# A gated add over 50 MB: loads in one order on one DMA ring, stores held back on the other

## The chip, the cores and the metric

The kernel runs on one core of a Trainium2 chip. Times are device microseconds of one execution; the kernel before takes 121.15 us, the median of 8 runs (120.98 to 121.7). The profile shows one such execution, taken by the hardware profiler, with times counted from its first instruction.

The core's engines that appear here are VectorE (DVE), which does the arithmetic, TensorE (PE), used once, and two engines that only issue transfers: SyncE (SP) and ScalarE (ACT). Each of the two has its own DMA ring, a queue of transfers between the chip's HBM and the core's SBUF. All transfers are carried by the same 16 DMA engines.

## The reference

```python
B, S, D = 1024, 16, 512
x = normal(B, S, D) * 0.05        # bf16
y = normal(B, S, D) * 0.05        # bf16
gamma = 1e-4 * normal(D) * 0.05   # bf16
out = x + gamma * y
```

x, y and the output have 16.78 MB each: two are read, one is written, 50.33 MB in all.

## The kernel before

The 16384 rows of 512 numbers are spread over 128 partitions, 128 consecutive rows (128 KB) to each. All of y has a place in SBUF (`y_sb`, 128 KB per partition). x has two buffers of 32 rows (32 KB per partition each). The work is cut into four pieces of 32 rows per partition; a piece of x, y or the output is one DMA of 4 MB. The result of a piece is written over its y, and stored from there.

First gamma is brought to all partitions: one row is loaded (line 65), TensorE multiplies it by a column of ones into PSUM (line 69), and VectorE copies it to SBUF (line 71).

Then VectorE runs two instructions per piece, in order: y times gamma (line 98), waiting for that piece of y, then x plus the product (line 104), waiting for that piece of x and for the product.

The order of the transfers is written out by hand, and each ring takes its transfers in that order:
- SP's ring: x of pieces 0 and 1 (lines 75, 76), which are put at the very start of the program; after the first add the reload of x for piece 2 (line 78), after the second add that for piece 3 (line 80), directly after it the store of piece 0 (line 81), and after the third add the store of piece 2 (line 83).
- ACT's ring: gamma, then y of all four pieces, without a wait (line 87); after the second add the store of piece 1 (line 91), after the fourth the store of piece 3 (line 93).

Waits go through semaphores; `_take` (line 12) waits for a count and takes it off again. A DMA adds 16 to its semaphore when it has landed. At the end SP waits for the stores of both rings (lines 115, 116). Loads all go through the helper on line 62, so the profile shows them with that line. The profile's q1 is SP's ring, q10 is ACT's.

Of the kernel before, what the change touches and what calls it, by code (L numbers as in the profile page):

```python
# [3 lines left out]

PIECE = 32
MULT, ADD = mybir.AluOpType.mult, mybir.AluOpType.add


def _take(sem, n, eng):


    return eng.wait_ge(sem, n).then_inc(sem, -n)  # L12


def kernel(
    tc: tile.TileContext,
    x: bass.AP,
    y: bass.AP,
    gamma: bass.AP,
    out: bass.AP,  # L20
):

    nc = tc.nc
    P = nc.NUM_PARTITIONS
    tc.close()
    tc.compile()  # L29

    xf = x.flatten_outer_dims()
    yf = y.flatten_outer_dims()
    of = out.flatten_outer_dims()
    N, D = xf.shape
    rows = N // P
    n = rows // PIECE
    dt = xf.dtype
    xv = xf.rearrange("(p n) d -> p n d", p=P)
    yv = yf.rearrange("(p n) d -> p n d", p=P)
    ov = of.rearrange("(p n) d -> p n d", p=P)  # L40

    gamma_row = nc.alloc_sbuf_tensor("gamma_row", [1, D], dt).ap()
    ones_row = nc.alloc_sbuf_tensor("ones_row", [1, P], dt).ap()
    gamma_sb = nc.alloc_sbuf_tensor("gamma_sb", [P, D], dt).ap()
    y_sb = nc.alloc_sbuf_tensor("y_sb", [P, rows, D], dt).ap()
    xs = [nc.alloc_sbuf_tensor(f"x{i}", [P, PIECE, D], dt).ap() for i in range(2)]
    gamma_ps = nc.alloc_psum_tensor("gamma_ps", [P, D], mybir.dt.float32).ap()

    sem = nc.alloc_semaphore
    s_gamma, s_ones, s_ps, s_dve = sem("s_gamma"), sem("s_ones"), sem("s_ps"), sem("s_dve")  # L50
    s_x = [sem(f"s_x{c}") for c in range(n)]
    s_y = [sem(f"s_y{c}") for c in range(n)]
    s_sp, s_act = sem("s_sp"), sem("s_act")
    s_out_sp, s_out_act = sem("s_out_sp"), sem("s_out_act")

    def piece(c):
        return slice(c * PIECE, (c + 1) * PIECE)

    first = []

    def load(eng, dst, src, s):
        return eng.dma_start(out=dst, in_=src).then_inc(s, 16)


    first.append(load(nc.scalar, gamma_row, gamma.unsqueeze(0), s_gamma))
    nc.vector.memset(ones_row, 1.0).then_inc(s_ones, 1)  # L66
    _take(s_ones, 1, nc.tensor)
    _take(s_gamma, 16, nc.tensor)
    nc.tensor.matmul(gamma_ps, ones_row, gamma_row, start=True, stop=True).then_inc(s_ps, 1)  # L69
    _take(s_ps, 1, nc.vector)  # L70
    nc.vector.tensor_copy(out=gamma_sb, in_=gamma_ps).then_inc(s_dve, 1)  # L71
    _take(s_dve, 1, nc.vector)


    first.append(load(nc.sync, xs[0], xv[:, piece(0), :], s_x[0]))
    first.append(load(nc.sync, xs[1], xv[:, piece(1), :], s_x[1]))
    _take(s_sp, 1, nc.sync)
    load(nc.sync, xs[0], xv[:, piece(2), :], s_x[2])
    _take(s_sp, 1, nc.sync)
    load(nc.sync, xs[1], xv[:, piece(3), :], s_x[3])  # L80
    nc.sync.dma_start(out=ov[:, piece(0), :], in_=y_sb[:, piece(0), :]).then_inc(s_out_sp, 16)
    _take(s_sp, 1, nc.sync)
    nc.sync.dma_start(out=ov[:, piece(2), :], in_=y_sb[:, piece(2), :]).then_inc(s_out_sp, 16)


    for c in range(n):
        i = load(nc.scalar, y_sb[:, piece(c), :], yv[:, piece(c), :], s_y[c])
        if c < 2:
            first.append(i)
    _take(s_act, 1, nc.scalar)  # L90
    nc.scalar.dma_start(out=ov[:, piece(1), :], in_=y_sb[:, piece(1), :]).then_inc(s_out_act, 16)
    _take(s_act, 1, nc.scalar)
    nc.scalar.dma_start(out=ov[:, piece(3), :], in_=y_sb[:, piece(3), :]).then_inc(s_out_act, 16)

    for c in range(n):
        yt = y_sb[:, piece(c), :]
        _take(s_y[c], 16, nc.vector)
        nc.vector.tensor_tensor(  # L98
            out=yt, in0=yt, in1=gamma_sb[:, None, :].to_broadcast([P, PIECE, D]), op=MULT
        ).then_inc(s_dve, 1)  # L100
        _take(s_x[c], 16, nc.vector)
        _take(s_dve, 1, nc.vector)

        i = nc.vector.tensor_tensor(out=yt, in0=xs[c % 2], in1=yt, op=ADD)  # L104
        if c == 0:
            i.then_inc(s_sp, 1)
        elif c == 1:
            i.then_inc(s_dve, 1)
            _take(s_dve, 1, nc.vector)
            nc.vector.sem_inc(s_sp, 1)  # L110
            nc.vector.sem_inc(s_act, 1)
        else:
            i.then_inc(s_sp if c == 2 else s_act, 1)

    _take(s_out_sp, 32, nc.sync)
    _take(s_out_act, 32, nc.sync)

    main = nc.main_func.blocks[0].instructions
    names = {i.ins.name for i in first}
    for b in nc.main_func.blocks[1:]:  # L120
        for i in [i for i in b.instructions if i.name in names]:
            b.instructions.remove(i)
    for k, i in enumerate(first):
        main.insert(1 + k, i.ins)


# [1 line left out]
_INS = ['x', 'y', 'gamma']  # L128
_OUTS = [((1024, 16, 512), 'bfloat16')]


# [23 lines left out]
```

## Time and profile before

| what | value |
|---|---|
| median of 8 runs | 121.15 us (120.98 to 121.7) |
| the profiled execution's own time | 121.46 us |
| its span, first to last instruction | 120.1 us |
| VectorE busy | 70.3 us (59%) in 10 instructions |
| one multiply, one add (128 x 16384, bf16) | 8.69 us each, four of each |
| moved by DMA | 50.33 MB, mean 419 GB/s over the span |
| VectorE idle before its first multiply | 18.2 us |

How to read it: a page of the profile lists busy time by engine, then the span in 40 equal slices, where each digit is the busy share of a slice in tenths, then the DMA queues with their packets, megabytes and share of the 16 DMA engines' time. Other views give the instructions in order of time, the busy times and transfer rate in stretches that one names, and the DMA queues of a stretch. Instructions that issue a DMA are shown with the time of the issue alone, and transfers are seen in the DMA rows.

### The profile page before, as it was taken

How to read it: one execution, taken by the hardware profiler on the slowest of the kernel's cores; microseconds unless marked ns; L12 is line 12 of the kernel's file. 1: busy time of each engine (PE TensorE's matmuls, PEld its weight loads, DVE VectorE, ACT ScalarE, POOL GpSimd, SP SyncE). 2: the span in 40 equal slices, each digit the busy share in tenths (PEclk: the TensorE clock that was granted, in tenths of full speed). 3: DMA queues.
4: the chain of work that ended last, by engine and by line, in shares of the span. 5: the costliest groups of instructions: out<-in, count | busy, mean ns of one | idle time of the engine just before them, and what ended most of it. 6: DMA issues, size and time to landing. Idle time of an engine off the chain costs nothing. (4 is left out here: it accounts for less than half of the span.)

```text
span 120.1 us, 90 instructions
## 1 busy us (share of the span) xinstructions
PE 0.6 (0%) x1; PEld 0.1 (0%) x1; DVE 70.3 (59%) x10; POOL 0.2 (0%) x4
## 2 busy tenths in 40 slices
PE   0100000000000000000000000000000000000000
PEld 0000000000000000000000000000000000000000
DVE  0200000099999999999899999899999700000000
POOL 0000000000000000000000000000000000000000
DMA  8999998989898989898989999999999999999994
GB/s 306 393 447 426 426 447 382 491 371 502 360 513 349 524 349 524 349 513 360 491 382 458 415 426 327 426 393 480 393 480 393 469 404 469 393 458 415 436 436 186
DMA packets 1730, 50.33 MB, mean 419 GB/s; under 512 B 193, under 2 KB 194, under 8 KB 194
## 3 DMA queue, kind: packets, MB, share of 16 engines
q1 hardware_dynamic: 864, 25.17, 49.7%
q10 hardware_dynamic: 866, 25.17, 48.7%
HBM read 33.56 MB, written 16.78 MB: 419 GB/s over the span
## 5 line engine op out<-in xcount | busy, mean ns | idle before, releaser
L98 DVE TENSOR_TENSOR y_sb<-y_sb,gamma_sb 128x16384 bf16<-128x16384 bf16 x4 | 34.8, 8690 | 19.2 <-DVEq L12 19.2
L104 DVE TENSOR_TENSOR y_sb<-x,y_sb 128x16384 bf16<-128x16384 bf16 x4 | 34.8, 8692 | 0.6
L71 DVE CAST gamma_sb<-gamma_ps 128x512 bf16<-128x512 f32 x1 | 0.7, 692 | 2.5 <-DVEq L12 2.5
L66 DVE MEMSET ones_row<- 1x128 bf16 x1 | 0.2, 165 | 2.7 <-PEq L29 2.7
L69 PE MATMUL gamma_ps<-gamma_row,ones_row 1*128 1x512 bf16 x1 | 0.6, 577 | 4.6 <-PEq L12 4.6
L69 PEld LDWEIGHTS gamma_ps<-gamma_row,ones_row 1*128 1x128 bf16 x1 | 0.1, 99 | 4.6 <-issue 4.6
L139 POOL MEMSET const-bfloat16-1.0<- 128x1 bf16 x1 | 0.1, 101 | 0.0
L139 POOL MEMSET const-uint8-127<- 128x1 uint8 x1 | 0.1, 101 | 0.0
L139 POOL MEMSET const-float32-0.0<- 128x1 f32 x1 | 0.1, 98 | 0.2 <-issue 0.2
L139 POOL MEMSET const-float32-1.0<- 128x1 f32 x1 | 0.1, 98 | 0.0
## 6 DMA issues: line engine op xcount, KB each, us to landing
x<-in_x_dram SPq DMA_DIRECT2D x4, 4096.0 KB, 24.7
y_sb<-in_y_dram ACTq DMA_DIRECT2D x4, 4096.0 KB, 47.2
out_dram<-y_sb ACTq DMA_DIRECT2D x2, 4096.0 KB, 30.4
out_dram<-y_sb SPq DMA_DIRECT2D x2, 4096.0 KB, 42.3
gamma_row<-in_gamma_dram ACTq DMA_DIRECT2D x1, 1.0 KB
```

The costliest lines, as they stand in the source:

```text
L66: nc.vector.memset(ones_row, 1.0).then_inc(s_ones, 1)
L69: nc.tensor.matmul(gamma_ps, ones_row, gamma_row, start=True, stop=True).then_inc(s_ps, 1)
L71: nc.vector.tensor_copy(out=gamma_sb, in_=gamma_ps).then_inc(s_dve, 1)
L98: nc.vector.tensor_tensor(out=yt, in0=yt, in1=gamma_sb[:, None, :].to_broadcast([P, PIECE, D]), op=MULT).then_inc(s_dve, 1)
L104: i = nc.vector.tensor_tensor(out=yt, in0=xs[c % 2], in1=yt, op=ADD)
L139: nc = _bacc.Bacc("TRN2", target_bir_lowering=False, num_devices=1)
```

## The change

The lists at the top of the file now say what goes where. Rows are counted per partition, of 128.

- Loads go on SP's ring alone, as four of 64 rows (64 KB per partition, 8 MB each): y rows 0 to 63, x rows 0 to 63, y rows 64 to 127, x rows 64 to 127. The first two are at the start of the program. There is one x buffer of 64 rows, as large as the two before; the last load writes over the first x, and so SP waits before it for the adds of pieces 0 and 1.
- Stores go on ACT's ring alone, after gamma: rows 0 to 63 in one DMA of 8 MB, then rows 64 to 95, then rows 96 to 127. The first waits for `s_go`, and each waits for the adds of its rows.
- VectorE's order is now multiply 0, multiply 1, add 0, add 1, multiply 2, multiply 3, go, add 2, add 3. Its pieces still have 32 rows. `go` waits for the open multiplies and raises `s_go`; in the code it stands ahead of the third add.
- One semaphore counts the adds, with waits that don't take it down until the end; one counts all stores, waited for at 48.

The diff, cut to its core:

```diff
-PIECE = 32
+PIECES = [32, 32, 32, 32]
+SP = [('y', 0, 64), ('x', 0, 64, 0), ('y', 64, 128), ('x', 64, 128, 0)]
+ACT = [('g',), ('s', 0, 64), ('s', 64, 96), ('s', 96, 128)]
+EARLY = (2, 1)
+DVE = [('m', 0), ('m', 1), ('a', 0), ('a', 1), ('m', 2), ('m', 3), ('go',), ('a', 2), ('a', 3)]
...
-    xs = [nc.alloc_sbuf_tensor(f"x{i}", [P, PIECE, D], dt).ap() for i in range(2)]
+    x_rows = max(w[3] + w[2] - w[1] for w in x_loads)
+    x_sb = nc.alloc_sbuf_tensor("x_sb", [P, x_rows, D], dt).ap()
...
+    def frees(w):
+        old = x_loads[: x_loads.index(w)]
+        old = [v for v in old if meets(v[3], v[3] + v[2] - v[1], w[3], w[3] + w[2] - w[1])]
+        return [c for v in old for c in pieces_of(v[1], v[2])]
...
+    def ring(eng, what, n_early):
+        known, went = 0, False
+        for k, w in enumerate(what):
+            kind = w[0]
+            need = frees(w) if kind == "x" else pieces_of(w[1], w[2]) + list(w[3:]) if kind == "s" else []
+            need = max((order[c] + 1 for c in need), default=0)
+            if kind == "s" and not went and ("go",) in DVE:
+                _take(s_go, 1, eng)
+                went = True
+            if need > known:
+                eng.wait_ge(s_add, need)
+                known = need
...
+            elif kind == "x":
+                to = x_sb[:, w[3] : w[3] + w[2] - w[1], :]
+                i = eng.dma_start(out=to, in_=xv[:, w[1] : w[2], :]).then_inc(s_load[w], 16)
+            elif kind == "y":
+                r = slice(w[1], w[2])
+                i = eng.dma_start(out=y_sb[:, r, :], in_=yv[:, r, :]).then_inc(s_load[w], 16)
+            else:
+                r = slice(w[1], w[2])
+                i = eng.dma_start(out=ov[:, r, :], in_=y_sb[:, r, :]).then_inc(s_out, 16)
...
+    ring(nc.sync, SP, EARLY[0])
+    ring(nc.scalar, ACT, EARLY[1])
...
+    for kind, *args in DVE:
+        if kind == "go":
+            if open_mults:
+                _take(s_dve, open_mults, nc.vector)
+                open_mults = 0
+            nc.vector.sem_inc(s_go, 1)
+            continue
...
+        if kind == "m":
+            need(y_loads, c)
+            g = gamma_sb[:, None, :].to_broadcast([P, PIECES[c], D])
+            nc.vector.tensor_tensor(out=yt, in0=yt, in1=g, op=MULT).then_inc(s_dve, 1)
+            open_mults += 1
         else:
+            need(x_loads, c)
+            if open_mults:
+                _take(s_dve, open_mults, nc.vector)
+                open_mults = 0
+            at = x_at(starts[c])
+            xt = x_sb[:, at : at + PIECES[c], :]
+            nc.vector.tensor_tensor(out=yt, in0=xt, in1=yt, op=ADD).then_inc(s_add, 1)
+
+    nc.scalar.sem_inc(s_end, 1)
+    _take(s_end, 1, nc.sync)
+    _take(s_add, n, nc.sync)
+    _take(s_out, 16 * len(stores), nc.sync)
```

`order` gives the place of a piece's add among the adds, so the last load waits for a count of 2, and the three stores for 2, 3 and 4. `need` in the VectorE part waits once for each load that meets the piece.

## The prediction

> **What bounds the kernel now.** I read the page's slices and DMA queues first, then the transfer rate in stretches between the kernel's events, then the order in time of VectorE's steps and DMA issues, and last the DMA queues of one short stretch.
>
> The page's busy slices and its DMA queues:
>
> ```profile
> DVE  0200000099999999999899999899999700000000
> ...
> DMA  8999998989898989898989999999999999999994
> ...
> q1 hardware_dynamic: 864, 25.17, 49.7%
> q10 hardware_dynamic: 866, 25.17, 48.7%
> HBM read 33.56 MB, written 16.78 MB: 419 GB/s over the span
> ```
>
> The reader is to see that the 16 DMA engines are full from the first slice to the last, half for each ring (q1 is SP's, q10 ACT's), while VectorE is idle in the first and the last fifth. The page's chain holds only 7% of the span: transfers are not on it, so it can't carry the argument.
>
> The rate in chosen stretches (last column GB/s; a packet counts where it begins):
>
> ```profile
> 0.00:5.70 5.70, 0.58 (x1) 0.10 (x1) 0.51 (x2) 0.20 (x4) 1.00 0.94 368
> 5.70:22.65 16.95, 0.00 (x0) 0.00 (x0) 0.34 (x1) 0.00 (x0) 1.00 1.00 433
> 22.65:39.60 16.95, 0.00 (x0) 0.00 (x0) 15.18 (x2) 0.00 (x0) 1.00 1.00 433
> 40.80:45.64 4.84, 0.00 (x0) 0.00 (x0) 4.84 (x2) 0.00 (x0) 1.00 1.01 433
> 46.90:71.10 24.20, 0.00 (x0) 0.00 (x0) 23.46 (x4) 0.00 (x0) 1.00 1.01 433
> 72.30:78.30 6.00, 0.00 (x0) 0.00 (x0) 5.42 (x2) 0.00 (x0) 1.00 0.94 339
> 78.60:95.50 16.90, 0.00 (x0) 0.00 (x0) 16.58 (x2) 0.00 (x0) 1.00 1.01 434
> 102.60:117.10 14.50, 0.00 (x0) 0.00 (x0) 0.00 (x0) 0.00 (x0) 1.00 1.00 434
> ```
>
> The kernel runs at one rate, 433 GB/s, reading, mixed or writing. 50.33 MB / 433 GB/s = 116.24 us. One place falls out: 72.3 to 78.3 loses (433 - 339) / 433 x 6.0 = 1.30 us. It is where ACT's ring passes from its last load to the first store of the kernel; no view says why. SP's last wait ends at 120.04, so head and tail (first issue to full rate, last byte to semaphore) are together 120.04 - 116.24 - 1.30 = 2.5 us. By the first stretch the head is some 1.8 of it: 2.10 MB had begun by 5.70, are through about 6.6, and need 4.84 at full rate.
>
> VectorE and the issues in time (start, us):
>
> ```profile
> 24.27 8.69 DVE L98 TENSOR_TENSOR y_sb<-y_sb,gamma_sb 128x16384 bf16<-128x16384 bf16 x1 [18.23 <-DVEq L12]
> 33.11 8.69 DVE L104 TENSOR_TENSOR y_sb<-x,y_sb 128x16384 bf16<-128x16384 bf16 x1
> 41.72 8.69 DVE L98 TENSOR_TENSOR y_sb<-y_sb,gamma_sb 128x16384 bf16<-128x16384 bf16 x1
> 41.91 17.92 SPq L62 DMA_DIRECT2D x<-in_x_dram  x2
> 50.55 8.69 DVE L104 TENSOR_TENSOR y_sb<-x,y_sb 128x16384 bf16<-128x16384 bf16 x1
> 59.60 0.35 ACTq L91 DMA_DIRECT2D out_dram<-y_sb  x1
> ```
>
> Two steps without a dependence follow each other in 8.61 us (33.11 to 41.72), so a pair takes 8.61 + 8.69 = 17.30. From the first add's end (41.80) to SP's reload is 0.11; from the second's (59.24) by way of VectorE's own increments to ACT's store 0.36. From the landing of the first y (24.1: its issue at 0.69, and the y tile's shortest time to landing, 23.4) to its multiply are 0.1 to 0.2; I take 0.15.
>
> The queues from SP's reload of x at 41.91 to 45.2:
>
> ```profile
> q10 hardware_dynamic: 35, 1.15, 81.0%
> ...
> x<-in_x_dram SPq DMA_DIRECT2D x1, 4096.0 KB, 23.4
> ```
>
> SP's transfer was issued, and for 3.3 us only ACT's ring moved bytes. It cost nothing, because the other ring had work. This cover is what the change removes.
>
> **What the Trainium skill says.** "DMA: Bandwidth & Descriptors", Issuing engines are not separate DMA queues: both rings run on the same 16 engines. The trace agrees: 433 GB/s with ACT's ring alone (40.8 to 45.64) and with both. The same page, Where 436 GB/s comes from, gives a ceiling of 435.2; the trace is 0.5% under it. The same page, Queues, rings and completion order: an engine takes descriptors of a ring in order and alternates between rings that have work, so one ring alone has nothing to alternate with when it runs dry. "Perfetto Trace Analysis", DMA Instruction — HWDGE (DVE, Sync): the profiled issue ends when descriptors are made, and the semaphore comes after the data are confirmed; here the issue is 0.33 us and the landing 23.4.
>
> **The change part by part.** *Bytes and VectorE steps:* unchanged, 116.24 us of transfer, eight steps of 8.69. *Descriptors:* loads and the first store run 64 KB per partition. If all that parts 433 from 435.2 is a cost per descriptor, 0.5% of 116.24 = 0.58 us, and five sixths of the bytes halve theirs, the most to be had is 0.24 us (an estimate from that page); the least is nothing; I take 0.1. *One load ring:* y half, x half, y half are queued from the start, with no waits. The fourth load reuses the x buffer and waits in SP for two adds; behind it on SP stand only the final waits. With head + tail = 2.5 and 8.39 MB / 433 = 19.37 us a half:
> - y half lands 2.5 + 19.37 = 21.9; multiplies 22.0 to 39.3, before x half lands at 41.24. Adds from 41.39 to 58.69; SP issues the last load at 58.80.
> - The second y half is through at 1.8 + 58.11 = 59.9 (lands 60.6). If the last load needs the whole head again, it is at full rate from 60.60: **a gap of 0.69 us**. In one line: 2.5 + 0.15 + 17.30 + 0.11 - 19.37.
> - Second multiplies 60.76 to 78.06, go, ACT issues its first store at 78.42; with a head of 1.8 it is at rate at 80.22, while the last load is through at 60.60 + 19.37 = 79.97: **0.25 us more**. Together 0.94.
> - Last load lands 80.67; adds to 89.5 and 98.1. Their stores queue behind 19.37 us of the first store (80.2 to 99.6), and the last quarter starts by 109: 11 us of cover; gone, each us of lateness would count in full.
>
> *Stores held back:* the first store waits for go, after the second pair of multiplies (code order: before the third add). Behind that wait on ACT are only stores. It stops no load, but no store can fill either gap: in the kernel before, the other ring did. *Stall of 1.30 at the first store:* not explained, so bounded: gone (0) or kept (1.30). All loads still precede the first store, as here nearly all did, so I keep it. *One semaphore, fewer increments, final waits:* a few waits that end long before the last bytes; the last still waits for the last landing. Nothing. *Gamma:* first on ACT, now beside one ring; its matmul ran at 4.63, and the first multiply is due at 22.0: hidden by 17 us.
>
> Sum: 1.8 + 116.24 + 0.94 + 1.30 + 0.7 - 0.1 = 120.88 against 120.04 before: **+0.8 us**. The profiled execution took 121.46, 0.31 over the median of the runs (121.15), so I add to the median: **121.9 us**, own range 121.5 to 122.5.
>
> **Rivals.** *Hidden hand-overs (within 0.3%).* If the first packet is what counts and not the ramp, the head is 1.0 (the first load, issued at 0.00, begins to move bytes about then: 33 GB/s in the first microsecond, 492 in the second), the gaps shrink by 0.8 to 0.14, and the smaller descriptor count takes that back: 121.15. For: queued work on the same ring may start warm. Against: the issue comes only 1.1 us before the ring is dry. *The stall goes (faster).* If 72.3 to 78.3 was two rings meeting at the first store, a single ring passing over while the DMA is nearly empty doesn't pay it: 121.15 + 0.8 - 1.3 = 120.65. It decides as soon as the stall is gone and the gaps stay under about 1.0 (1.0 - 0.1 - 1.3 = -0.4). For: both rings were loaded there. Against: the rate was untouched at all other meetings. *Slow issue (much slower).* If the 3.4 us between 41.91 and SP's first packet is the issue itself and not a queue of ACT's packets ahead of it, the second hand-over comes at 2.5 - 1.8 + 3.4 + 0.15 + 17.30 + 0.36 - 19.37 = 2.5 us in all: 123.6. Against: the first load moved bytes within some 1 us of its issue.
>
> **How the numbers follow.** Chances: gaps with the stall kept 0.54; hidden 0.22; stall gone 0.13; slow issue 0.11. This kernel's measurement tells 0.3% (0.36 us) from no change. Faster 0.13, same 0.22, slower 0.54 + 0.11 = 0.65. The range runs from the faster rival, 120.6, to 122.9, somewhat over half way from the likeliest to the slow issue, since the head of a load and of a store onto a dry ring is only bounded (1.0 to 3.4 us). It leaves out the slow issue's 0.11 and some of the edges.
>
> **What would show it.** Right: all rate stretches 433 but for two dips, near 60 (0.7 us lost) and 80 (0.25 plus the stall); the third multiply at about 60.7, SP's last load at 58.8, the first store at 78.4, the last add ending near 98. Wrong: no dip near 60 (warm hand-over); no dip beyond the gap near 80 (stall gone); SP's queue empty for 2 us after 60 (slow issue); a rate other than 433 with one ring of 64 KB descriptors, which would move every line of the sum.

## The result and the profile after

The changed kernel takes 123.04 us (median; 122.44 to 124.14) against 121.15 us before (120.95 to 121.84): a ratio of 1.0158, with a 95% interval of 1.0135 to 1.0181. Slower was forecast, but by 0.8 us and not by 1.9, and the time lies above the range's 122.9. The profiled execution took 123.04, its span is 121.7 us; before it was 121.46 and 120.1.

The page of the changed kernel, its busy slices and DMA queues (q1 is SP's ring, q10 ACT's):

```profile
DVE  0020000799998399999399999706999990000000
...
DMA  9799779988998799779988999999898989898994
...
q1 hardware_dynamic: 576, 33.55, 65.4%
q10 hardware_dynamic: 434, 16.78, 32.4%
HBM read 33.56 MB, written 16.78 MB: 414 GB/s over the span
```

All loads are now on q1 and all stores on q10, and the mean rate has gone from 419 to 414 GB/s for the same bytes. The sevens in the DMA row say little here: a packet counts wholly in the slice where it begins, and one of 64 KB takes 2.42 us of the slice's 3.04. Rates over whole rounds of packets say more (last column GB/s):

```profile
5.70:22.65 16.95, 0.58 (x1) 0.10 (x1) 1.43 (x2) 0.00 (x0) 1.00 1.00 433
22.65:39.60 16.95, 0.00 (x0) 0.00 (x0) 16.55 (x2) 0.00 (x0) 1.00 1.01 433
...
65.00:77.10 12.10, 0.00 (x0) 0.00 (x0) 12.10 (x2) 0.00 (x0) 1.00 1.00 433
84.50:99.00 14.50, 0.00 (x0) 0.00 (x0) 14.50 (x2) 0.00 (x0) 1.00 1.00 434
102.60:117.10 14.50, 0.00 (x0) 0.00 (x0) 0.00 (x0) 0.00 (x0) 1.00 1.00 432
```

One ring of 64 KB packets runs at the 433 GB/s of the kernel before. So most of the loss is between these stretches. The order in time:

```profile
58.90 0.33 SPq L108 DMA_DIRECT2D x_sb<-in_x_dram  x1
60.96 17.29 DVE L150 TENSOR_TENSOR y_sb<-y_sb,gamma_sb 128x16384 bf16<-128x16384 bf16 x2 [2.09 <-DVEq L23]
78.52 22.27 ACTq L114 DMA_DIRECT2D out_dram<-y_sb  x3
83.13 17.29 DVE L159 TENSOR_TENSOR y_sb<-x_sb,y_sb 128x16384 bf16<-128x16384 bf16 x2 [4.88 <-DVEq L23]
```

The issue of the last load (58.80 forecast), the third multiply (60.76) and the first store (78.42) are within 0.2 us of the forecast. The third add is not: 83.13 where 80.8 was due, since by the trace's packet records the last packet of x ends only at 82.63. What happens at the hand-over, the passage from the second y half to the last load, is in the DMA view of 59 to 63, in bins of 0.1 us; 655 GB/s in a bin is one 64 KB packet that begins there, so 1966 is three:

```profile
GB/s 0 0 0 0 0 0 0 0 0 0 0 1966 1966 1311 655 1311 0 0 0 0 655 0 0 1311 0 0 655 655 0 0 0 0 0 0 0 0 0 0 0 0
```

Eleven of the 16 DMA engines begin the last load between 60.1 and 60.6, and five between 61.0 and 61.8, though all had finished the second y half by 60.53. A late engine stays late to the end. In the three traces of the changed kernel the last packet of x ends at 82.63, 83.04 and 83.41, and the last packet of all ends 38.7 us after it each time. That is one engine's share of the stores, 8 packets of 2.42 us and 16 of 1.21, with nothing taken over by the 15 others.

To compare the kernels I use the trace's packet records: the time at which so many MB had been moved, less those MB at 433 GB/s, gives a lag, and what the lag grows by in a stretch is what was lost there, averaged over the engines. The third column is how far the last engine's last packet ended behind the mean of the 16. All in us:

```
                              hand-over      turn to stores   last engine
                              24.6-27.3 MB   27.3-35.7 MB     behind the mean   span
before                          0.04           0.96             0.63            120.1
changed                         1.06           0.99             0.87            121.7
changed, second trace           1.14           0.82             1.75            122.1
changed, third trace            1.13           0.96             1.96            122.5
last load in two halves         0.01           0.51             0.56            119.4
  the same, second trace        0.00           0.66             0.37            119.4
8 rows as a bridge              0.03           0.73             0.49            119.6
all loads 32 rows               0.60           0.72             0.29            120.1
  the same, second trace        0.47           0.84             0.19            119.9
last load 2 us later            2.66           1.06             0.50            122.6
y half in 32 KB packets         0.92           1.01             1.95            122.4
x half in 32 KB packets         1.08           0.49             1.50            121.5
```

For the kernel before, the same bytes belong to other transfers: its first column is a stretch without a late hand-over. After 35.7 MB the lag grows in none of these runs, so the late third add cost nothing by itself. The three columns add up to the differences between the spans to within 0.2 us, but for the first trace of the changed kernel: there 0.3 us more went before 24.6 MB, where load packets took 2.45 us on the mean between 18 and 46 us, and 2.42 in the two other traces. It is no part of the hand-over, and its cause is open.

### The profile page after: what moved, and what is told of

Same layout as the page of the kernel before. It is cut to its first block, busy times and chain, and to the rows that moved or that the text cites. A ratio compares the mean times of both kernels' runs of the same rounds, so it can differ in the third digit from the quotient of the medians.

```text
span 121.7 us, 75 instructions
## 1 busy us (share of the span) xinstructions
PE 0.6 (0%) x1; PEld 0.1 (0%) x1; DVE 70.0 (58%) x10; POOL 0.2 (0%) x4
## 5 line engine op out<-in xcount | busy, mean ns | idle before, releaser
L159 DVE TENSOR_TENSOR y_sb<-x_sb,y_sb 128x16384 bf16<-128x16384 bf16 x4 | 34.6, 8688 | 7.2 <-DVEq L23 7.2
```

The source lines that it names most:

```text
L159: nc.vector.tensor_tensor(out=yt, in0=xt, in1=yt, op=ADD).then_inc(s_add, 1)
```

## The experiments

**The last load in two halves.** The hand-over is taken away: the reload of x is two DMAs of 32 rows, and each waits only for the add that frees its part of the buffer. The packets of that load are now of 32 KB too; what that does alone is tried further down (the incoming side).

```diff
-SP = [('y', 0, 64), ('x', 0, 64, 0), ('y', 64, 128), ('x', 64, 128, 0)]
+SP = [('y', 0, 64), ('x', 0, 64, 0), ('y', 64, 128), ('x', 64, 96, 0), ('x', 96, 128, 32)]
...
-        old = [v for v in old if meets(v[3], v[3] + v[2] - v[1], w[3], w[3] + w[2] - w[1])]
-        return [c for v in old for c in pieces_of(v[1], v[2])]
+        c = []
+        for v in old:
+            lo, hi = max(v[3], w[3]), min(v[3] + v[2] - v[1], w[3] + w[2] - w[1])
+            if lo < hi:
+                c += pieces_of(v[1] + lo - v[3], v[1] + hi - v[3])
+        return c
```

> The last load of 64 rows of x is cut in two DMAs of 32 rows: rows 64 to 95 are issued after the first add (about 50), rows 96 to 127 after the second (about 59). So SP's ring has 32 rows queued when the second y half ends near 60. Theory 1, the dry ring at that hand-over is what costs (about 0.65 us on every engine and about 1.9 on the slowest ones): about 121.2 us, within 0.3 us of the kernel before, and no dip in the rate between 59 and 63. Theory 2, one load ring with 64 KB descriptors, or the held stores, is what costs: it stays at 122.5 or more.

Measured: 120.83 us, ratio to before 0.9975 (0.996 to 0.9989). The same DMA view of 59 to 63, where a 32 KB packet is now 328 GB/s in a bin:

```profile
GB/s 0 0 0 0 0 0 0 1639 1966 983 328 328 0 0 0 0 0 0 0 1311 1638 1638 328 328 0 0 0 0 0 0 0 983 1966 1311 655 328 0 0 0 0
```

Sixteen packets every 1.21 us, and no engine is missing from a round. Theory 1 holds and theory 2 falls: one load ring, 64 KB packets in three quarters of the loads, held stores and all, is faster than the kernel before by 0.3 us, and the late hand-over with what follows from it costs 123.04 - 120.83 = 2.2 us. This version beats both kernels. Run again beside other kernels:

> The last load cut into two halves of 32 rows, each waiting for its own add, once more: if the cover of the hand-over is what counts, 120.8 within 0.3 on this chip as well, below the kernel before by 0.1 to 0.4%.

Measured: 120.84 us, ratio 0.9972 (0.9961 to 0.9983).

**How much cover it takes.** Only 8 of the 64 rows go ahead after the first add; the rule for what frees the buffer is that of the split.

```diff
+SP = [('y', 0, 64), ('x', 0, 64, 0), ('y', 64, 128), ('x', 64, 72, 0), ('x', 72, 128, 8)]
```

> The last load is cut into 8 rows (issued after the first add) and 56 rows (issued after the second, near 59). The 8 rows, 1 MB, are a bridge of 2.4 us over the hand-over. Theory 1 with an issue of 1.3 us to the first engine and 2.9 to the last, as the trace after has it: 121.2 to 121.6, the gap is covered or nearly. If a transfer needs 3.4 us from its issue or more, some 1 us of the gap stays: 122.2. Theory 2: 122.5 or more.

Measured: 120.89 us, ratio 0.9973 (0.9961 to 0.9985). 1 MB on the ring, 2.4 us of work, covers the hand-over wholly, and the time is 0.3 us under the lowest expected. The expectation that a start-up of 3.4 us, the prediction's slow issue, would show here was mistaken: the 56 rows are issued at 58.62, and the bridge's packets end between 62.1 and 62.5, so 3.4 us would be covered too. The next run decides it.

**The hand-over made later.** One more VectorE instruction stands between the second add and the reload.

```diff
+DVE = [('m', 0), ('m', 1), ('a', 0), ('a', 1), ('d',), ('m', 2), ('m', 3), ('go',), ('a', 2), ('a', 3)]
...
+            if kind == "x" and w[1] >= 64:
+                need = 3
...
+        if kind == "d":
+            g = gamma_sb[:, None, :].to_broadcast([P, 8, D])
+            nc.vector.tensor_tensor(out=scratch, in0=g, in1=g, op=MULT).then_inc(s_add, 1)
```

> VectorE does one more instruction after the second add, a product of gamma with itself into 8 scratch rows (about 2.2 us, its result isn't used), and SP's last load waits for it instead of the second add. So that load is issued 2.2 us later, and nothing else is due later. Theory 1: the hand-over's gap grows by the same, 125.2 us, and the ring is empty for 2 to 3 us after 60. Rival, the load has slack at the hand-over: about 123.0.

Measured: 124.08 us, ratio 1.023 (1.0207 to 1.0253); so 1.0 us over the changed kernel, not 2.2. The views of that run, order in time and then the DMA view of 59 to 63:

```profile
58.49 2.28 DVE L150 TENSOR_TENSOR scratch<-gamma_sb 128x4096 bf16<-128x4096 bf16 x1
...
60.80 0.33 SPq L111 DMA_DIRECT2D x_sb<-in_x_dram  x1
```

```profile
GB/s 0 0 0 0 0 0 0 0 0 0 0 0 0 0 0 0 0 0 0 0 0 0 0 0 0 0 0 3277 1966 3932 0 655 0 0 0 0 655 0 0 0
```

The issue came 1.9 us later, an engine stood idle for 2.0 us on the mean, and the loss at the hand-over grew by 1.5 to 1.6 (2.66 for 1.06 to 1.14). But 14 of the 16 engines now begin within 0.3 us (61.7 to 62.0), the other two by 62.2 and 62.7, and the last engine ends only 0.50 behind the mean. That is where the expected 2.2 went: the changed kernel already pays for engines left behind. From this run the price of a hand-over on an empty ring can be read: after the issue it takes 1.0 us to the first packet, 1.1 on the mean of the engines, and the first packet of each engine takes 0.6 us more than the later ones (3.05 for 2.42, mean). Together 1.8 us; the slow issue's 3.4 is not there.

**The size of the packets.** Every load of 64 rows becomes two DMAs of 32 rows, with all waits where they were.

```diff
+SP = [('y', 0, 32), ('y', 32, 64), ('x', 0, 32, 0), ('x', 32, 64, 32), ('y', 64, 96), ('y', 96, 128), ('x', 64, 96, 0), ('x', 96, 128, 32)]
+EARLY = (4, 1)
...
+            if kind == "x" and w[1] >= 64:
+                need = 2
...
+            half = starts[c] // 64 * 64
+            if w not in landed and meets(half, half + 64, w[1], w[2]):
```

> Every load of 64 rows is issued as two DMAs of 32 rows (32 KB per partition), but each wait stays where it was: VectorE waits for both halves, and both parts of the last x wait for the second add. Theory 1: the hand-over is unchanged, so 123.0 us within 0.4. Theory 2, the 64 KB descriptors read more slowly: 122.5 or less, and the packets' time in the loads goes back to 1.21 us per 32 KB.

Measured: 121.38 us, ratio 1.0026 (1.0006 to 1.0046). That is theory 2's number, but not its reason: the rate in the loads is the same 433 with packets of 32 or 64 KB. Theory 1 has the right reason and missed the number: the hand-over is as late as ever (issue at 58.76), and yet 1.7 us are gone. To see whether it was the chip, the same kernel was run once more, beside the changed kernel:

> All loads as DMAs of 32 rows, waits unchanged, once more, beside the changed kernel on one chip. Theory D, small packets on both sides of the hand-over leave no engine behind: 121.3 to 121.6 here too, and the changed kernel beside it 122.5 to 123.5. Theory C, what differed was the chip: both within 0.4 us of each other.

> The changed kernel beside the run before. Theory D: 122.5 to 123.5, one or more engines starting the last load over 0.8 us after their neighbours. Theory C: within 0.4 us of the run with 32-row DMAs.

Measured: 121.4 us, ratio 1.0019 (1.0009 to 1.0028; three executions of twelve, at 123.2 to 123.9, are not in the ratio), and 123.4 us, ratio 1.0174 (1.0124 to 1.0223). The difference comes from the edit, not from the chip. The edit makes the packets smaller and the DMAs twice as many; the runs don't tell these two apart. The DMA views of 59 to 63, first of the changed kernel's run (64 KB packets, 655 each), then of the first run with 32 KB packets (328 each):

```profile
GB/s 0 0 0 0 0 0 0 0 1966 1966 1311 655 655 0 655 0 0 0 0 1966 0 0 655 0 0 0 0 0 0 655 0 0 0 0 0 0 0 0 0 1966
```

```profile
GB/s 0 0 0 0 0 0 0 655 328 2294 983 655 0 0 0 328 0 0 0 0 0 0 0 0 0 328 1638 983 1638 328 328 0 0 0 0 0 0 328 1311 1311
```

Above, eleven engines begin by 60.5, four near 61 and one at 61.9. Below, all but one begin between 59.7 and 60.2 and that one at 60.5; what is left is the 0.5 to 0.6 us of the slow first packets. The late engine shows again at the end. The DMA view of 117 to 122 of the changed kernel's run (a store packet of 32 KB is 262 in a bin of 0.125 us):

```profile
GB/s 524 786 1311 262 262 0 0 786 262 0 1311 524 786 262 262 0 262 524 0 0 262 262 0 0 0 0 0 0 0 0 0 262 0 0 0 0 0 0 0 0
```

The last packet begins near 120.9, 1.2 us after the one before it: as it begins the other 15 engines have ended or are ending their last, and then the kernel waits for one. With small packets 18 executions of the first run took 121.2 to 121.6 and four 122.2 to 122.8, nine of the second 121.2 to 121.5 and three 123.2 to 123.9, so an engine may be left behind there too now and then; no trace was taken of such an execution, and that is only argued.

**Which side of the hand-over.** Small packets only in the outgoing second y half (first line below), or only in the incoming x (the others; both its DMAs wait for the second add), each beside the changed kernel.

```diff
+SP = [('y', 0, 64), ('x', 0, 64, 0), ('y', 64, 96), ('y', 96, 128), ('x', 64, 128, 0)]
...
+SP = [('y', 0, 64), ('x', 0, 64, 0), ('y', 64, 128), ('x', 64, 96, 0), ('x', 96, 128, 32)]
...
+            if kind == "x" and w[1] >= 64:
+                need = 2
```

> Of the changed kernel, only the second y half is issued as two DMAs of 32 rows, so the packets that run out at the hand-over near 60 are of 32 KB and those that come after it, the last x, still of 64 KB. All waits stand where they were. Theory A, an engine that is in a long packet when the late descriptors come starts them about 1 us late: about 121.5 us, and no engine is idle for more than 0.4 us near 60. Theory B, it is the incoming 64 KB packets that come late: about 123.0. Theory C, neither, the size of the hand-over changes from chip to chip: like the changed kernel run beside it.

> The mirror of the run before: the second y half is one DMA of 64 rows, the last x is two DMAs of 32 rows that both wait for the second add. Theory A: about 123.0 us, some engines idle for about 1 us near 60. Theory B: about 121.5. Theory C: like the changed kernel run beside it.

> The changed kernel once more, on the chip of the two runs before. Theories A and B: 123.0 within 0.5, with engines idle for 0.8 to 1.3 us near 60. Theory C: 121.5 to 122 here, without such engines.

Measured: outgoing 123.25 us (ratio 1.0141, 1.0086 to 1.0197), incoming 122.97 (1.0124, 1.0073 to 1.0175), the changed kernel 123.1 (1.014, 1.008 to 1.0199). Theories A and B both fall: neither side alone helps, and so the small incoming packets of the split are not what it gains by. In the packet records of the changed kernel's run all 16 engines have ended the y half by 60.31, and the last one begins x at 62.03, 1.72 us later; with one side small it is 1.20 and 1.09, with all loads small 0.36 and 0.35. The records don't name the engine of a packet, so which one is late, and whether it was the last out, can't be read from them. Why cutting all loads mostly avoids it stays open; no run cuts just the two loads at the hand-over.

**The held stores.** The split kernel without the go, so that the first store may be issued after the second add.

```diff
-DVE = [('m', 0), ('m', 1), ('a', 0), ('a', 1), ('m', 2), ('m', 3), ('go',), ('a', 2), ('a', 3)]
+DVE = [('m', 0), ('m', 1), ('a', 0), ('a', 1), ('m', 2), ('m', 3), ('a', 2), ('a', 3)]
```

> The kernel with the last load cut in two halves of 32 rows (120.83 us), and the go taken out: the first store, rows 0 to 63, is issued after the second add near 59 instead of near 78, so it alternates with the last load. If the hold is worth nothing, since the DMA engines have work either way: 120.8 within 0.4; the last load lands later (near 95) and the fourth add ends near 105, still ahead of its store's turn. If holding the stores is what pays: 121.5 or more, because the last store is issued with too little ahead of it.

Measured: 124.19 us, ratio 1.0229 (1.0188 to 1.027); so it is the holding of the stores that pays. Order in time, and the DMA view of 107 to 113 (a packet of 32 KB is 218 in a bin of 0.15 us):

```profile
58.73 53.19 ACTq L118 DMA_DIRECT2D out_dram<-y_sb  x3
...
88.17 8.69 DVE L163 TENSOR_TENSOR y_sb<-x_sb,y_sb 128x16384 bf16<-128x16384 bf16 x1 [10.22 <-DVEq L23]
102.86 8.69 DVE L163 TENSOR_TENSOR y_sb<-x_sb,y_sb 128x16384 bf16<-128x16384 bf16 x1 [6.00 <-DVEq L23]
```

```profile
GB/s 218 218 0 0 1092 1092 874 0 218 218 0 0 0 0 0 0 0 218 0 0 0 0 0 0 0 0 0 0 0 0 0 0 0 0 0 0 3277 218 0 0
```

The early store shares the DMA engines with the last load, whose last packet then ends at 102.4, before the fourth add begins at 102.86 (in the split kernel the loads are through at 79.5). That add ends at 111.55 (102.86 + 8.69), too late for its store's turn: 15 of the 16 DMA engines stand idle from about 109 to 112.4, and by the packet records 3.4 us are lost there. The hold is what keeps work ahead of the last store: without it the split kernel loses about 3 us (ratios 1.0229 and 0.9972).

**The stall at the first store.** The split kernel with one row per partition stored early, ahead of the go and of the rest of its half.

```diff
+ACT = [('g',), ('s', 0, 1), ('s', 1, 64), ('s', 64, 96), ('s', 96, 128)]
...
-            if kind == "s" and not went and ("go",) in DVE:
+            if kind == "s" and w[1] > 0 and not went and ("go",) in DVE:
```

> As the run before, but row 0 of each partition is stored alone (128 KB in all) after the second add, near 59, ahead of the go; the first held store is rows 1 to 63. If the stall at the first store (0.5 us an engine near 79 here, 1.0 near 74 in the kernel before) is paid once, by whatever store comes first, and a small one pays little: 120.4, and no slow packets near 79. If it belongs to the turn from loading to storing: 120.8 as the run beside it, slow packets near 79 remain.

Measured: 120.87 us, ratio 0.9971 (0.996 to 0.9981), as the split kernel beside it. The small store was issued at 50.36, after the first add and not the second as expected, since its row belongs to piece 0; its packets run from 54.8 to 66.7 among those of the loads. By the packet records nothing is lost there (0.02 us), and 0.4 still near 79, where the split kernel loses 0.5 to 0.7. So a small store doesn't take the price over, or little of it, and the time is the same.

## Why the prediction was wrong

*What bounds it, and the steady rate: right.* 433 GB/s with one ring or two, packets of 32 or 64 KB, loads or stores. The gain of 0.1 us taken for fewer descriptors is about what is there: in the split kernel, with packets of 64 KB, the lag falls by 0.08 us between 4.2 and 24.6 MB, and with 32 KB on the same ring it stays level.

*Where the gap comes: right.* The issue at 58.80 was 58.90; covering the hand-over gives all of the loss back. That VectorE's due times and a ring that runs dry decide this change was the right reading.

*The step that failed: the size of "a gap of 0.69 us".* It put one head of 1.8 us on all 16 engines alike. On a ring that is empty already the head is that (1.1 + 0.6 in the run with the later reload). On a ring just running dry, from issue to full rate, it was 2.1 to 2.4 on the mean of the engines in the three traces of the changed kernel, and the mean loss was 1.06 to 1.14 us. And the engines are not alike: up to five begin about 1 us after their neighbours, the last 1.3 to 1.7 us after all had become free, and the last to end is 0.87 to 1.96 us behind the mean (0.63 before). The last load lands when its slowest engine is through, and the kernel ends so too. Two terms, 0.4 us of mean and 0.2 to 1.3 of a left-behind engine, are what the sum lacked. That the time of one kernel spreads from 122.44 to 124.14 would follow from how far the worst engine falls behind; this is argued from three traces, whose spans of 121.7, 122.1 and 122.5 go with that column and end 38.7 us of packets after their last x packet.

*The stall (1.30, kept): right to keep, though too large. The second gap (0.25): not there.* The turn to stores lost 0.82 to 0.99 us in all, against 0.96 by the same records in the kernel before (the 1.30 read from a 6 us stretch was 0.3 too much, since a packet counts where it begins). So it adds nothing to the difference, where the prediction had 0.25; without that error the forecast would have been further off. In the split kernel, where the hand-over is clean, the turn costs 0.5 to 0.7.

*"It stops no load": the hold.* It was booked as costless, and as taking away the cover by stores. That it is worth about 3 us (measured on the split kernel), because it keeps stores from slowing the loads that VectorE waits for, was not seen.

*The rivals.* Hidden hand-overs: shown wrong here, but true of the bridge and the split, which land 0.3 us below before. The stall gone: wrong. Slow issue: named for the right place and nearer in time (123.6), wrong in mechanism: with the ring idle, the first packet begins 1.0 us after the issue and the last engine's 1.9, not 3.4. Longer times were seen only with the other ring full: the 3.4 in the kernel before, and 4.5 for the small early store (50.36 to 54.8). The chance of 0.65 for slower came out; the range ended 0.1 us short, and its centre took the engines as one.

## What to carry to other kernels

When the DMA engines are full all the time, ask of each wait on a ring what is queued behind it or on the other ring while the wait's transfer starts; 1 MB of cover was worth 2.2 us here. Split a reload so that each part waits only for what frees it. Price a transfer on a ring that runs dry by its slowest engine, not by a mean start-up. Hold back stores when they would slow loads that the arithmetic waits for and the last store would then come late.

## What the runs showed of the hardware that was not expected

- When a load is issued on an empty ring, first packets begin about 1.0 us after the issue and take about 0.6 us longer than later ones (3.05 us for 2.42 at 64 KB), as at the kernel's start. The last store of the run without the go also met idle engines: its packets begin 0.85 us after the issue (111.58, 112.43) and take 1.22 from the first, no longer than the rest.
- If the late issue falls in the last packets of the transfer before, the last engine begins 1.1 to 1.7 us after all 16 were free, in five traces with 64 KB packets on at least one side of the hand-over; with 32 KB in all loads 0.36 and 0.35 in the two traces taken.
- The first turn from loads to stores costs 0.4 to 1.1 us on the mean of the engines, in all kernels with held stores here and in the kernel before.
